# A first block loaded in two halves, its neighbour's statistics on another engine, and a new order of work

## The chip, the cores and the metric

The kernel runs on one core of a Trainium2 chip. Five engines work side by side, each through its own list of instructions in order: TensorE (PE; its weight loads are listed apart as PEld), VectorE (DVE), ScalarE (ACT), GpSimd (POOL) and SyncE (SP), which issues most of the DMA transfers. They wait for each other through semaphores. The metric is the device time of one execution in microseconds (us), the median of several runs.

## What is computed

A layer norm over rows of 640 values feeds two branches, which are added to the input:

```python
x = A_x                                        # (1, 2048, 640)
xn = _layernorm(x, axis=-1)
return x + _A_ref(xn, A_wqkv, A_wo) + _B_ref(xn, B_w1, B_b1, B_w2, B_b2)
```

Branch A is attention with 32 heads of 20 values. Each position sees eight positions: itself and those 2, 4, ... 14 before it; softmax over these eight, weighted sum of the values, then the projection `wo`. Branch B is a dense layer of width 1536 with bias and the tanh form of GELU, and a second dense layer with bias back to 640. Inputs, weights and output are bf16.

## The kernel before

**Tiling.** The 2048 rows are four chunks n = 0..3 of 512 columns (`CH`), each of four blocks of 128 rows (`BPC`). `x_sb` holds the input, block by block. A block is normalised, transposed, and gathered with its neighbours in `xnT`, 5 x 128 features by 512 rows, the moving operand of all projections.

**Layer norm.** Chunks 0 and 1 take mean and variance on VectorE: two half statistics of 320 columns each and one aggregate (`do_st`, L213 and L215). Chunks 2 and 3 take them on ScalarE: a sum (`do_su`, L225), its negative mean (`do_ng`, L229) and a sum of squares (`do_sq`, L232). Block 1 of chunk 0 is taken on ScalarE too, in the pieces `sum1`, `neg1` and `sq1`. `do_rs` (L244, L247) makes the reciprocal root by a logarithm and an exponential on ScalarE. `do_xn` (L264) normalises, for blocks 0 and 1 in two parts of 256 (a) and 384 (b) columns. `do_tp` (L279) transposes on TensorE and `do_tc` (L284) copies the result to `xnT`, on VectorE for block 0 and the first part of block 1, else on ScalarE. From chunk 1 on a DMA transposes (`do_td`, L291).

**Projections.** Chunk 0's are in small pieces: `ga`, `gb2`.. (block 0) and `gd`, `ge` (block 1) for the queries at 128 columns (L346), `hj...` for pairs of blocks at 256 columns (L377), with their copies out of PSUM on ScalarE (`gc.`, `hc...`, L392). Later chunks use `pj` and `pc` at 512 columns (L333, L397).

**Attention.** VectorE multiplies queries with keys (`qk`, L430), folds, and TensorE sums over the values of a head (`lg`, L480). After the softmax SP spreads the weights over partitions by DMA (`xe`, L574), VectorE multiplies with the values (`av`, L581), folds by itself or by an accumulating DMA (`ac`, L592 and L594; `ad`, L598), and writes `oT` (`ot`, L604).

**Dense branch and output.** `f1` (L611) are five matmuls of the hidden layer into one of the four PSUM accumulators of the pool `psA`, `ge` (L627) the GELU. `t` (L690) accumulates the second layer and `wo` for chunks 0 to 2, in parts 0..3 (hidden) and 4 (`wo`); `u` adds the bias, `ut` transposes by DMA, `ud` adds to the output by an accumulating DMA. Chunk 3 is computed the other way round (`o`, L646), with x added by VectorE (`dl`, `dh`) and written in `dd`, `dlo`, `dhi`. Before that `xp` writes x of a whole chunk to the output.

**Order.** The list `ORDER` names every piece of work, and all five engines get their instructions in that order: what stands earlier in the list stands earlier on its engine. It is written out by hand; nothing is reordered afterwards. Loads at the start stand ahead of it: SP issues block 0, the query weights, blocks 2 and 3, the key weights, chunk 1, the value weights and the two halves of w1; ScalarE issues block 1 and the two bias vectors. `ldx` loads the later chunks, `ld2` w2 and `ldo` wo. `tb` (L453) turns the biases on TensorE and `b1` (L456) copies them out. DMA transfers from SP and ScalarE take turns at eight semaphores; a transfer is issued when the eighth before it has landed.

**Warm-up.** Ahead of the list TensorE runs `WARM` matmuls of 512 columns and three of 128 on constants (`do_warm`, L443); the pieces `wa` and `wb` are three more between the first transposes.

Of the kernel before, what the change touches and what calls it, by code (L numbers as in the profile page):

```python
# [29 lines left out]
WARM = 10  # L30
# [13 lines left out]
hj110 xn13 hc112 hj012 tc13 xn11 hj200 hc010 hc110 tc11 qk00 hj011 hc200 hc012 hj201 hc011 xn10 f10_1 hc201 qk02 tc10  # L44
xn12 f10_11 tc12 f10_2 ldx ge0_1 f10_5 qk03 ge0_11 ge0_2 f10_3 ge0_5 f10_0 pad11 ge0_3 pa00 pj103 ge0_0 pj100 pc103
pa01 su20 xp2 pj110 pc100 ld2 pj101 pc110 su22 pb01 pj104 su21 pj102 pc101 su23 pb04 pj114 pc104 ng2 pc102 pj112 ldo
sq22 sq21 lg0 pj111 cp0b cp0a pc112 pj113 mask m0b pc111 pc114 m0a xp1 hj211 pc113 mx0b xp0 mx0a hj210 qk13 ex0a pj122
ex0b hc210 pj123 sq23 ss0b t040 pc122 ss0a sq20 pj124 qk12 hc211 t000 rs2 pc123 f10_4 ri0a pc124 pj120 ri0b at0a rc2
qk11 f10_6 pj121 ge0_4 xn23 f10_7 xn21 qk10 tc23 t041 ge0_6 t001 tc21 pc121 su33 f10_8 pc120 at0b f11_9 su32 pa10 xe00
ge0_7 f11_1 xn20 f11_3 ge0_8 tc20 pa11 xn22 f11_10 ge1_1 tc22 ge1_9 t042 pb11 su31 xe03 t002 xe02 hj202 f10_9 xe01  # L50
hc202 ge1_10 pb14 su30 f10_10 ge0_9 pj203 ge0_10 lg1 pc203 pj210 cp1a av00 cp1b f11_5 ng3 sq32 f11_0 pc210 ge1_5 av01
pj202 ac00 ge1_0 hj212 pc202 pj212 sq30 m1 hc212 pj211 ac01 ge1_3 sq31 av03 t003 pad12 pj222 pc211 pc212 pad21 pj201
mx1 pj220 av02 ex1 t043 pc201 pj224 sq33 pj204 ss1 pc220 pc224 f12_6 pc222 ac03 ri1 pj223 at1 pj214 pc223 ac02 xe10
pc204 pj200 xe13 rs3 pc214 xe12 ad00 pad22 pj213 pc200 xe11 rc3 ad01 f11_6 pc213 xn33 pj221 ot00 xn30 tc33 ot01 f11_8
av10 t004 tc30 t044 u00 t010 av13 u04 ut00 t011 xn32 t012 xn31 tc32 t013 ud00 t014 av11 tc31 ac10 t030 u01 t031 pc221
t032 t033 ac13 ac11 t034 av12 f11_7 t020 t021 ge2_6 t022 ge1_6 ac12 t023 ge1_8 t024 u03 ut01 ad11 f12_9 ot11 pj303
ge2_9 qk22 f11_2 f11_4 ge1_2 pc303 pj301 qk23 ge1_4 f11_11 t130 ge1_11 t131 ad10 ge1_7 f12_2 u02 pc301 ut02 pa21 t140
pad31 ge2_2 pj300 ut03 pj311 ot10 ut04 ud01 f12_3 qk21 pc311 pc300 f13_2 ud02 pj312 xb qk20 pj314 pc312 ud03 pj302
pc314 ge2_3 pj313 pa20 pj304 t132 pc304 pb21 t133 pc302 t134 t141 u13 pb24 f13_5 pj310 ge3_5 ge3_2 lg2 t142 cp2a t143
cp2b t100 pc310 m2 pad32 f13_4 pc313 mx2 t101 qk30 f13_3 ex2 t144 f13_0 ss2 u14 f13_1 qk33 t102 ge3_3 ge3_1 t103 ge3_4  # L60
t110 f13_10 qk31 t104 ri2 f13_8 qk32 ge3_0 pj322 u10 f12_10 ge3_10 t111 at2 ge2_10 f12_8 pa31 pc322 xe22 ut10 f13_6
t112 pa30 f12_5 xe21 xe23 t113 ge2_5 xe20 t120 pb31 ge3_8 f12_0 ge3_6 ge2_8 t114 pb34 f12_4 u11 ut11 ud10 pj321 lg3
pj324 cp3b av21 ge2_4 t121 pc324 t122 cp3a pj323 m3 ac21 f12_7 pc323 mx3 ge2_0 t123 ge2_7 av20 o300 pc321 f13_9 f12_1
ex3 av23 ac20 f13_11 t124 ge2_1 pj320 ac23 u12 ge3_9 ut12 ud11 ud04 f13_7 pc320 ss3 ge3_11 t200 ge3_7 t230 av22 t231
f12_11 ri3 o301 at3 o302 ac22 xe33 ge2_11 t201 xe32 t202 xe31 ad21 t203 ut13 o320 ot21 t232 ad20 o310 o311 ut14 ot20
o312 av33 t204 t233 u20 t234 ut20 av32 t210 u23 ud12 xe30 t211 t212 t213 av31 t220 t221 t214 t222 ac31 u21 t223 t224
av30 t240 u22 ud13 ud20 ut21 ud14 t241 t242 t243 ac30 o330 t244 ac32 o321 u24 ud21 ut22 ad30 ud22 ut23 o331 ut24 o313
ot30 o322 ac33 o303 ud23 o304 ad31 o314 ud24 ot31 dh0 o323 dh1 dl1 o324 dl0 dd1 dd0 o332 dl2 o333 dh2 dd2 o334 ohi dl3
dlo dh3 dhi
# [4 lines left out]
def kernel(  # L74
# [50 lines left out]
    def load_x(b0, b1):  # L125
        nc.sync.dma_start(x_sb[:, b0:b1, :], x_nb[:, b0:b1, :])  # L126
# [12 lines left out]
    load_w(2)  # L139
    for c in range(2):  # L140
        cs = slice(c * F // 2, (c + 1) * F // 2)
        nc.sync.dma_start(w1_sb[:, :, cs], w1_v[:, :, cs])
# [67 lines left out]
    def do_st(n, bl, i):  # L210
# [3 lines left out]
        if i:  # L214
            nc.vector.bn_aggr(mv[:, b, :], stats[:])  # L215
# [635 lines left out]
```

## Time and profile before

| what | us |
|---|---|
| median of 3 runs | 205.6 |
| the runs | 205.41, 205.6, 207.96 |
| the profiled execution | 205.49 |
| its span, first to last instruction | 203.3 |

The span is the part of the execution in which the program's instructions ran; 2.19 us of the profiled execution lie around it. The page gives the busy time of each engine and its share of the span, then the span in slices, the DMA queues, the chain of work that ended last, and the costliest groups of instructions. A busy engine off the chain costs nothing. In a row such as `L611 PE MATMUL hps<-xnT,w_sb ... x240`, L611 is the line of the kernel, `hps` what is written, what follows the arrow what is read; in brackets stands the idle time of the engine before it and what ended that.

### The profile page before, as it was taken

How to read it: one execution, taken by the hardware profiler on the slowest of the kernel's cores; microseconds unless marked ns; L12 is line 12 of the kernel's file. 1: busy time of each engine (PE TensorE's matmuls, PEld its weight loads, DVE VectorE, ACT ScalarE, POOL GpSimd, SP SyncE). 2: the span in 40 equal slices, each digit the busy share in tenths (PEclk: the TensorE clock that was granted, in tenths of full speed). 3: DMA queues.
4: the chain of work that ended last, by engine and by line, in shares of the span. 5: the costliest groups of instructions: out<-in, count | busy, mean ns of one | idle time of the engine just before them, and what ended most of it. 6: DMA issues, size and time to landing. Idle time of an engine off the chain costs nothing.

```text
span 203.3 us, 2874 instructions
## 1 busy us (share of the span) xinstructions
PE 199.4 (98%) x1100; PEld 105.0 (52%) x1100; DVE 185.8 (91%) x159; ACT 129.7 (64%) x237; POOL 29.5 (14%) x35
## 2 busy tenths in 40 slices
PE   8999999999999999999999999999999999999994
PEld 3899455654454555444444544444444445444552
DVE  2899999899997999999999996999979999999981
ACT  5689979999979897555545437697447990211100
POOL 3000000000000400024202500000202702253420
PEclk9999999999999999999999999999999999999999
DMA  6996399940673681849912890001863898895951
GB/s 204 390 395 208 77 355 336 348 148 3 91 155 89 110 148 22 219 92 163 193 17 52 102 99 5 3 0 15 170 98 69 153 118 147 111 120 90 103 90 64
DMA packets 38430, 27.31 MB, mean 134 GB/s; under 512 B 25106, under 2 KB 34578, under 8 KB 38418
## 3 DMA queue, kind: packets, MB, share of 16 engines
q1 hardware_dynamic: 28016, 20.29, 38.2%
q0 software_dynamic: 10080, 6.56, 26.3%
q10 hardware_dynamic: 322, 0.30, 0.4%
q8 instruction: 8, 0.13, 0.3%
q14 instruction: 4, 0.03, 0.0%
HBM read 10.49 MB, written 4.59 MB: 74 GB/s over the span
## 4 chain that ended last, share of the span: by engine, by line
PE 96%; DMA 2%; SPq 0%; DVE 0%; issue 0%
PE T L690 27%; PE hps L611 25%; PE pps L333 24%; PE lo L646 7%; PE gps L377 7%; DMA wq_sb<-in_A_wqkv_dram 2%; PE hi L646 2%; PE gps L346 1%; PE L L480 1%; PE tp L279 0%; SPq L126 0%; DVE prod L658 0%; PE tb L453 0%
## 5 line engine op out<-in xcount | busy, mean ns | idle before, releaser
L611 PE MATMUL hps<-xnT,w_sb 128*128 128x512 bf16 x240 | 56.9, 379 | 0.0
L430 DVE TENSOR_TENSOR prod<-qT,kT 128x5120 bf16<-128x5120 bf16 x16 | 44.5, 2820 | 0.1
L690 PE MATMUL T<-hT,w_sb 128*128 128x512 bf16 x180 | 43.4, 379 | 0.0
L611 PEld LDWEIGHTS <-w_sb 128*128 128x128 bf16 x240 | 23.5, 98 | 27.5
L702 POOL DMA_DIRECT2D out_dram<-x_sb x15 | 20.9, 1492 | 87.5 <-DMA x_sb<-x_sb 87.5
L627 ACT ACTIVATE hT<-hps,bT 128x512 bf16<-128x512 f32 x36 | 23.9, 689 | 12.1 <-PE hps L611 9.6
L690 PEld LDWEIGHTS <-w_sb 128*128 128x128 bf16 x180 | 17.5, 98 | 21.1 <-issue 0.4
L693 ACT ACTIVATE x_sb<-T,bT 128x512 bf16<-128x512 f32 x15 | 10.3, 688 | 25.6 <-PE T L690 24.5
L581 DVE TENSOR_TENSOR prod<-vT,ax 128x5120 bf16<-128x5120 bf16 x8 | 22.4, 2820 | 2.7 <-PE L L480 1.5
L581 DVE TENSOR_TENSOR prod<-vT,x_sb 128x5120 bf16<-128x5120 bf16 x8 | 22.2, 2817 | 0.0
L592 POOL DMA_DIRECT2D prod<-prod x6 | 7.8, 1300 | 77.5 <-DVE prod L581 77.5
L170 ACT ACT_TABLE_LOAD x14 | 18.0, 1283 | 1.0 <-PEq L835 0.7
L471 DVE TENSOR_TENSOR prod<-prod 128x4096 bf16<-128x4096 bf16 x8 | 18.3, 2291 | 0.3
L333 PE MATMUL pps<-xnT,wv_sb 128*128 128x512 bf16 x75 | 18.5, 379 | 0.0
L690 PE MATMUL T<-oT,wo 128*128 128x512 bf16 x75 | 18.5, 379 | 0.0
L333 PE MATMUL pps<-xnT,wq_sb 128*128 128x512 bf16 x75 | 18.1, 379 | 0.0
L465 DVE TENSOR_TENSOR prod<-prod 128x4096 bf16<-128x4096 bf16 x8 | 18.0, 2286 | 0.0
L333 PE MATMUL pps<-xnT,wk_sb 128*128 128x512 bf16 x75 | 18.0, 380 | 0.0
L594 DVE TENSOR_TENSOR prod<-prod 128x2560 bf16<-128x2560 bf16 x10 | 14.8, 1487 | 0.1
L333 PEld LDWEIGHTS <-wq_sb 128*128 128x128 bf16 x75 | 8.8, 117 | 7.5
L333 PEld LDWEIGHTS <-wv_sb 128*128 128x128 bf16 x75 | 8.7, 118 | 7.6 <-issue 0.4
L333 PEld LDWEIGHTS <-wk_sb 128*128 128x128 bf16 x75 | 8.6, 118 | 7.7 <-issue 0.8
(91 smaller groups left out, 242.6 us busy)
## 6 DMA issues: line engine op xcount, KB each, us to landing
prod<-prod POOLq DMA_DIRECT2D x6, 640.0 KB, 6.8
ax<-attn SPq DMA_DIRECT2D x8, 256.0 KB, 3.9
x_sb<-attn SPq DMA_DIRECT2D x8, 256.0 KB, 4.5
w_sb<-in_B_w_dram SPq DMA_DIRECT2D x2, 960.0 KB, 11.0
out_dram<-x_sb SPq DMA_DIRECT2D x3, 640.0 KB, 6.8
w_sb<-in_B_w_dram SPq DMA_DIRECT2D x4, 480.0 KB, 6.6
out_dram<-x_sb POOLq DMA_DIRECT2D x15, 128.0 KB, 5.6
x_sb<-in_A_x_dram SPq DMA_DIRECT2D x2, 640.0 KB, 7.0
```

What stands on the lines that cost most here:

```text
L170: nc.scalar.preload_act_table_set(name)
L333: nc.tensor.matmul(ps[:], lhsT=wqkv_p[which][:, ti, to, :], rhs=xnT[:, ti, :], start=(ti == 0), stop=(ti == KT - 1),)
L430: nc.vector.tensor_tensor(out=prod[:, j], in0=q[:, :, at].unsqueeze(1).to_broadcast([P, W, KT, P]), in1=window(k, at), op=ALU.mult,)
L465: nc.vector.tensor_tensor(out=low, in0=low, in1=high, op=ALU.add)
L471: nc.vector.tensor_tensor(out=first, in0=first, in1=rows[:, :, t * P : (t + 1) * P], op=ALU.add)
L581: nc.vector.tensor_tensor(out=prod[:, j], in0=window(qkv_tile(n, 2), slice(j * P, (j + 1) * P)), in1=ax_view(n)[:, j, :, :].unsqueeze(2).t ...
L594: nc.vector.tensor_tensor(out=low, in0=low, in1=high, op=ALU.add)
L611: nc.tensor.matmul(ps[:], lhsT=w1_sb[:, ti, ft * P : (ft + 1) * P], rhs=tiles["xnT", n][:, ti, :], start=(ti == 0), stop=(ti == KT - 1),)
L627: nc.scalar.activation(hT, tiles["hps", n, ft][:], ACT.Gelu_apprx_tanh, bias=bT[:, ft : ft + 1], scale=1.0)
L646: nc.tensor.matmul(out_ps(bl, hi), lhsT=lhs, rhs=rhs[:, CH:D] if hi else rhs[:, 0:CH], start=pc == 0 and k == 0, stop=pc == 4 and k == len ...
L690: nc.tensor.matmul(ps[:], lhsT=lhs, rhs=rhs, start=pc == 0 and k == 0, stop=pc == 4 and k == len(srcs) - 1)
L702: nc.gpsimd.dma_start(dst, src, accum_op=ALU.add)
```

## The change

- Block 0 is loaded in two transfers of 320 columns each, both from SP.
- Block 1's statistics are taken on VectorE like its neighbours': the pieces `sum1`, `neg1`, `sq1` go, `st01a`, `st01` and, on its own in the order, the aggregate `ag01` come. Its normalisation subtracts the mean as the others do.
- The two bias loads move from ScalarE's queue to SP's, behind the value weights.
- Block 0's second copy to `xnT` and block 1's first move from VectorE to ScalarE.
- w2 is loaded in three transfers instead of four.
- The hidden matmuls of chunk 0 are split into pieces of two and three (`f10_..a`, `f10_..b`), which accumulate into the same tile.
- Nine warm-up matmuls instead of ten.
- Another order. Its first lines, and the stretches in which the attention weights of chunk 0 are spread, are shown; the rest is a different interleaving of the same pieces.

```diff
-WARM = 10
+WARM = 9
 ORDER = """
-pad01 pad02 st00a st00 sum1 rs00 neg1 xn00a sq1 xn00b tp00a wa tp00b tc00a wb rs01 tc00b ga xn01b gb2 xn01a tp01b
-st03a tp01a tb tc01b gb3 tc01a gb4 st03 gd gc0 st02a ge rs03 st02 hj101 xn03 rs02 gc1 xn02 tp03 gc4 st12a tp02 tc03
-hj100 st13a st13 tc02 st12 hj102 hc101 st11a hj111 hc100 st10a hc102 st11 hj010 st10 hc111 ho b1 rs1 hj112 pk rc1 qk01
+pad02 pad01 st00a st00 st01 rs00 xn00a st01a tp00a wa wb xn00b ag01 tc00a tp00b rs01 ga tc00b xn01a xn01b gb2 st03a
+tp01a tp01b gb3 st03 tc01a gb4 tc01b gd st02a rs03 st02 ge ho xn03 rs02 hj101 gc0 xn02 gc1 tp02 gc4 tp03 st13a hc101
+hj102 st11a tc03 st11 hj100 tc02 st13 st12a hj010 hc100 st12 hc102 st10a tb hj110 st10 hc010 b1 rs1 hj012 hc110 rc1
...
-qk11 f10_6 pj121 ge0_4 xn23 f10_7 xn21 qk10 tc23 t041 ge0_6 t001 tc21 pc121 su33 f10_8 pc120 at0b f11_9 su32 pa10 xe00
-ge0_7 f11_1 xn20 f11_3 ge0_8 tc20 pa11 xn22 f11_10 ge1_1 tc22 ge1_9 t042 pb11 su31 xe03 t002 xe02 hj202 f10_9 xe01
+hj202 ge0_8 f10_6a tc20 f10_6b xn23 t001 hc202 tc23 ge1_1 f10_10a at0a pa11 f10_10b ge0_6 f11_3 ge0_10 xn22 f10_9a
+pa10 f10_9b xn21 tc22 f11_9 tc21 f11_10 ge1_9 at0b pb11 xe00 t002 ge1_10 xe03 pj124 ge1_3 xe01 su33 pj121 pb14 su32
+xp1 t042 su31 xe02 pj203 ge0_9 pc121 lg1 su30 hj212 av00 t003 ng3 pc124 pj212 cp1b hc212 pc203 f11_5 sq32 av01 ac00
...
-    load_x(0, 1)
+    for cs in (slice(0, D // 2), slice(D // 2, D)):
+        nc.sync.dma_start(x_sb[:, 0, cs], x_nb[:, 0, cs])
     nc.scalar.dma_start(x_sb[:, 1, :], x_nb[:, 1, :])
-    nc.scalar.dma_start(b_rt[0:FT, :], B_b1.rearrange("(t p) -> t p", p=P))
-    nc.scalar.dma_start(b_rt[FT : FT + KT, :], B_b2.rearrange("(t p) -> t p", p=P))
     load_w(0)
     load_x(2, BPC)
     load_w(1)
     load_x(BPC, 2 * BPC)
     load_w(2)
+    nc.sync.dma_start(b_rt[0:FT, :], B_b1.rearrange("(t p) -> t p", p=P))
+    nc.sync.dma_start(b_rt[FT : FT + KT, :], B_b2.rearrange("(t p) -> t p", p=P))
...
-        for c in range(4):
-            ts = slice(c * FT // 4, (c + 1) * FT // 4)
+        for c in range(3):
+            ts = slice(c * FT // 3, (c + 1) * FT // 3)
...
-        if i:
-            nc.vector.bn_aggr(mv[:, b, :], stats[:])
+        if i and b != 1:
+            do_ag(b)
+
+    def do_ag(b):
+        nc.vector.bn_aggr(mv[:, b, :], tiles["stats", b][:])
...
-            scalar1=neg[:, 1:2] if bl == 1 else mv[:, i, 0:1],
+            scalar1=mv[:, i, 0:1],
             scalar2=rstd[:, i : i + 1],
-            op0=ALU.add if bl == 1 else ALU.subtract,
+            op0=ALU.subtract,
             op1=ALU.mult,
...
-    def do_f1(n, ft):
-        ps = psA.tile([P, CH], F32, tag="acc", name="hps")
-        tiles["hps", n, ft] = ps
-        for ti in range(KT):
+    def do_f1(n, ft, a=0, b=KT):
+        ps = get(("hps", n, ft), lambda: psA.tile([P, CH], F32, tag="acc", name="hps"))
+        for ti in range(a, b):
...
-    for u, a, b, eng in (("a", 0, 2, "ve"), ("b", 2, KT, "se")):
+    for u, a, b, engs in (("a", 0, 2, ("ve", "se")), ("b", 2, KT, ("se", "se"))):
         for bl in range(2):
             piece(f"xn0{bl}{u}", do_xn, 0, bl, a, b)
             piece(f"tp0{bl}{u}", do_tp, 0, bl, a, b, True)
-        piece(f"tc00{u}", do_tc, 0, 0, a, b, "ve")
-        piece(f"tc01{u}", do_tc, 0, 1, a, b, eng)
+        for bl in range(2):
+            piece(f"tc0{bl}{u}", do_tc, 0, bl, a, b, engs[bl])
```

The later lines of the order end alike, with `ohi dl3 dlo dh3 dhi`.

More of the change, by code (lines that the diff above doesn't have):

```diff
@@ new lines @@
+pj202 cp1a sq30 pj201 pc212 pc202 pj214 ge1_5 m1 ac01 sq31 t043 av03 pc201 f11_0 pc214 pj200 ge1_0 pj222 mx1 av02
+pj211 ex1 pj210 pc211 pad12 pc200 pj221 ss1 sq33 pj213 pc221 ac02 pc210 pj223 ri1 rs3 at1 pj220 pc213 rc3 ac03 xe12
+pc222 xn30 pj224 xe11 xe13 ad00 pc223 f11_7 pc220 xn31 ad01 f11_4 pc224 tc31 f12_6 ot00 ot01 pj204 tc30 av12 t004
+pc204 xe10 t044 u00 pad21 xn32 t010 av13 t011 u04 ut00 xn33 t012 t013 tc33 ud00 t030 av11 t014 tc32 t031 u01 t032 t020
+av10 ac11 t021 ge1_4 f11_11 t022 ge1_11 ac13 t033 ac10 ge1_7 t034 ac12 xb t023 u03 ut01 t024 ad11 pj303 ot11 f11_2
@@ L70 @@
+t224 o313 ad31 u22 ud13 ud20 ut21 ud14 t240 av31 t241 t242 o330 t243 t244 ac30 o331 u24 ud21 ut22 ud22 ut23 ac31 o320
+ut24 o321 ot31 o322 ud23 ad30 o323 o324 ot30 ud24 o303 dh2 o314 o304 dl1 dl2 o332 dh1 dd2 dh0 dl0 o333 dd1 dd0 o334
+ohi dl3 dlo dh3 dhi
 """.split()
@@ L241, in do_rs @@
         sl = slice(n * BPC + b0, n * BPC + b1)
-        summed = n in ACT_STATS or (n, b0) == (0, 1)
         table(LOG_SET)
         nc.scalar.activation(
-            logv[:, sl], mv[:, sl, 1], ACT.Ln, bias=eps_t[:], scale=1.0 / D if summed else 1.0
+            logv[:, sl], mv[:, sl, 1], ACT.Ln, bias=eps_t[:], scale=1.0 / D if n in ACT_STATS else 1.0
         )
@@ L720 @@
             piece(f"tp0{bl}{u}", do_tp, 0, bl, a, b, True)
-        piece(f"tc00{u}", do_tc, 0, 0, a, b, "ve")
-        piece(f"tc01{u}", do_tc, 0, 1, a, b, eng)
+        for bl in range(2):
+            piece(f"tc0{bl}{u}", do_tc, 0, bl, a, b, engs[bl])
     for bl in range(BPC):
-        if bl != 1:
-            piece(f"st0{bl}a", do_st, 0, bl, 0)
-            piece(f"st0{bl}", do_st, 0, bl, 1)
+        piece(f"st0{bl}a", do_st, 0, bl, 0)
+        piece(f"st0{bl}", do_st, 0, bl, 1)
         piece(f"rs0{bl}", do_rs, 0, bl, bl + 1)
@@ L791 @@
         for ft in range(FT):
-            piece(f"f1{n}_{ft}", do_f1, n, ft)
+            if n:
+                piece(f"f1{n}_{ft}", do_f1, n, ft)
+            else:
+                piece(f"f1{n}_{ft}a", do_f1, n, ft, 0, 2)
+                piece(f"f1{n}_{ft}b", do_f1, n, ft, 2, KT)
             piece(f"ge{n}_{ft}", do_ge, n, ft)
```

44 lines of the change are left out of this document (17 added, 27 removed).

## The prediction

> **What bounds the kernel now.** I read the page's busy times and its chain first, then the busy times by window, then the first microseconds engine by engine, then the places where another engine hands work to TensorE.
>
> ```profile
> PE 199.4 (98%) x1100; PEld 105.0 (52%) x1100; DVE 185.8 (91%) x159; ACT 129.7 (64%) x237; POOL 29.5 (14%) x35
> ...
> PE 96%; DMA 2%; SPq 0%; DVE 0%; issue 0%
> ```
>
> TensorE (PE) is busy for 98% of the span and makes up 96% of the chain that ended last; VectorE (DVE) is second at 91%. By stage (window, its length, then busy time of PE, weight loads, DVE, ScalarE and GpSimd; the last figure is GB/s of the DMA engines):
>
> ```profile
> 0.00:6.31 6.31, 5.17 (x21) 2.10 (x22) 2.19 (x7) 3.82 (x9) 1.53 (x13) 1.00 0.71 238
> 6.31:200.60 194.29, 194.24 (x1079) 102.93 (x1079) 183.31 (x152) 125.92 (x229) 27.93 (x22) 1.00 0.66 132
> 200.60:203.30 2.70, 0.00 (x0) 0.00 (x0) 0.29 (x1) 0.00 (x0) 0.00 (x0) 0.89 0.20 61
> sum 203.30, PE 199.41 PEld 105.04 DVE 185.79 ACT 129.74 POOL 29.46; mean PE 66.47 PEld 35.01 DVE 61.93 ACT 43.25 POOL 9.82
> ```
>
> From 6.31 to 200.60 PE idles for 0.05 us in all. So the time is a head of 6.31 us, 194.3 us of PE work without a hole, and a tail of 2.7 us. The change takes none of that work away: the one matmul that goes is a warm-up on constants in the head. A gain can come only from the head or the tail, and the last steps of the tail stand in both orders alike; a loss comes as a later head or as a hole in the middle. Two per cent of 205.6 us is 4.1 us, about what a measurement of this kernel can tell from no change.
>
> What ends the head, from the chain in order of time (start, length, what):
>
> ```profile
> 1.19 5.07 DMA wq_sb<-in_A_wqkv_dram
> 6.27 0.05 issue
> 6.31 1.03 PE gps L346 x15
> ...
> 9.64 1.09 PE gps L377 x10
> 10.73 0.56 PE tp L279 x10
> ```
>
> The first real matmuls wait for the query weights, issued at 1.19 and landed at 6.26.
>
> **The head, step by step.** SP's own rows, VectorE's, ScalarE's and those of PE's weight loads (start, length, engine, line, operation, and in brackets the idle time before it and its releaser):
>
> ```profile
> 0.74 0.39 SPq L126 DMA_DIRECT2D x_sb<-in_A_x_dram  x1
> 1.19 0.42 SPq L129 DMA_DIRECT2D wq_sb<-in_A_wqkv_dram  x1
> ...
> 3.65 0.85 SPq L129 DMA_DIRECT2D wv_sb<-in_A_wqkv_dram  x1
> 6.28 2.23 SPq L142 DMA_DIRECT2D w_sb<-in_B_w_dram  x2
> ```
>
> ```profile
> 3.27 0.89 DVE L213 BATCH_NORM_STATS2 stats<-x_sb 128x6 f32<-128x320 bf16 x2 [3.27 <-DMA x_sb<-in_A_x_dram]
> 4.19 0.21 DVE L215 BATCH_NORM_AGGREGATE mv<-stats 128x2 f32<-128x12 f32 x1
> 5.07 0.63 DVE L264 TENSOR_SCALAR xn<-x_sb,mv,rstd 128x256 bf16<-128x256 bf16 x2 [0.66 <-ACT rstd L247]
> 5.79 0.70 DVE L284 COPY xnT<-tp 128x256 bf16<-128x256 bf16 x2
> ```
>
> ```profile
> 3.65 0.74 ACT L225 ACTIVATE trash<-x_sb 128x640 bf16<-128x640 bf16 x1 [1.63 <-DMA x_sb<-in_A_x_dram]
> 4.29 0.19 ACT L225 ACTIVATION_READ_ACCUMULATOR trash<-x_sb 128x1 f32 x1
> 4.50 0.29 ACT L244 ACTIVATE logv<-mv,eps_t 128x1 f32<-128x1 f32 x1
> ...
> 7.55 0.48 ACT L284 COPY xnT<-tp 128x384 bf16<-128x384 bf16 x1 [0.91 <-PE tp L279]
> ```
>
> ```profile
> 4.15 0.15 PEld L443 LDWEIGHTS <-const-bfloat16-1.0 128*128 128x128 bf16 x1 [0.28 <-issue]
> ...
> 6.31 0.77 PEld L346 LDWEIGHTS <-wq_sb 128*128 128x128 bf16 x13 [0.28 <-DMA wq_sb<-in_A_wqkv_dram]
> ```
>
> *Two column halves.* No row shows a load of half a block. The whole block, issued at 0.74, let the statistics begin at 3.27, 2.53 later. The first half carries half the bytes and can hardly be later; the second is issued one place later, by the step from 0.74 to 1.19, 0.45. It lands between 3.27 (the same bytes by the same time) and 3.72. Before, the second statistic began half of 0.89 after the first, at about 3.7; now it begins between 3.5 (the first half at best some 0.25 sooner) and 3.75. I take 3.6, nearer to the whole block's row. ScalarE gains a little as well: block 1's sum and its read-out held it until 4.48, while the aggregate was there at 4.40, so the logarithm starts some 0.05 sooner. Block 0's first normalised columns come at 5.07 - 0.15 = 4.9, with bounds of 4.75 and 5.05.
>
> The Trainium skill's page "DMA: Bandwidth & Descriptors", section "Anatomy of one DMA", speaks against halving: about 2.0 us fixed for each transfer, plus bytes / 436e3, fitted on the gpsimd path. That makes an estimate of 2.4 us for the 160 KB block (the trace has 2.53 to its first use) and 2.2 for a half: the second half would be there at 3.4, and the head below would come out 0.15 shorter.
>
> *The query weights, one issue later.* They go out at about 1.64. If the landing follows the issue, it moves from 6.26 to 6.71; if the transfers ahead of it keep the DMA engines busy anyway, it stays. The engines moved 238 GB/s averaged over the whole head, its idle start included, against 132 over the rest, so I lean to the second and take 6.4.
>
> *Block 1's statistics on VectorE.* ScalarE's sum and square go; VectorE gets two half statistics (0.45 each) and an aggregate (0.21). The first half statistic stands before the normalisation, inside VectorE's wait of 0.66, and is free while that wait lasts (0.45 if it went). The other half statistic and the aggregate stand between the first normalisation and the copy that fills xnT: 0.66 in line. From the start of the normalisation to the end of the first copy it took 5.79 + 0.35 - 5.07 = 1.05 and will take 1.7, so the copy ends at 4.9 + 1.7 = 6.6, with bounds of 6.45 and 6.75. So a new wait, for VectorE's copy, comes 0.2 behind the weights. First projection at 6.6 instead of 6.31: +0.3.
>
> *The second copy moves to ScalarE*, behind block 1's logarithm and exponential. Those wait for the aggregate (6.25), take 0.55 up to what reads them (from 4.50 to 5.07), and the copy 0.48: columns at 7.3. Ten of the fifteen projections (1.03 for 15) cover 6.6 to 7.3. No further loss, 0.1 at most.
>
> *Warm-up.* A warm-up matmul steps at 0.15 + 0.28 = 0.43 us; one less is worth nothing, since PE waits behind them for the normalised columns. The second rival has its other side.
>
> Sum of the head: +0.3, with bounds of -0.05 (the weights at 6.26) and +0.45.
>
> **Moves that should cost nothing.** The bias loads leave ScalarE's queue for SP's, behind the value weights and ahead of w1. Landing times by issue:
>
> ```profile
> w_sb<-in_B_w_dram SPq DMA_DIRECT2D x2, 960.0 KB, 11.0
> ...
> wv_sb<-in_A_wqkv_dram SPq DMA_DIRECT2D x1, 800.0 KB, 9.3
> ```
>
> The value weights land at 3.65 + 9.3 = 12.95, the biases (17 rows of 128 values) behind them, by my estimate between 13.0 and 13.6. The matmul that turns them has been moved behind four groups of key and query matmuls and ten transposes: from 9.64, 35 x 0.109 (1.09 for 10) + 0.56 = 4.4, so to 14.0 and with the later head 14.3. PE does not wait; if the biases came as late as w1 does, PE would wait up to 3 us there. w1's issue waited until 6.28, when the query weights had landed; two short issues fit in front of that. w1's second half is now used first, at about 20; the halves land 11.0 after issue in the median, about 17.3, and with an issue up to 1.1 later 18.4. The hidden projections of the first chunk split into 2 + 3 matmuls, the same number; one accumulator of four is held longer at one place, which I price at nothing to 0.2. w2 in three loads moves the same bytes.
>
> **The middle.** The new order is another interleaving; only waits decide. The tightest place that I find is the spreading of the first attention weights by SP:
>
> ```profile
> 53.44 0.68 SPq L574 DMA_DIRECT2D ax<-attn  x1
> 55.13 2.59 SPq L291 DMA_TRANSPOSE xnT<-xn  x2
> ```
>
> ```profile
> 63.31 5.56 DVE L581 TENSOR_TENSOR prod<-vT,ax 128x5120 bf16<-128x5120 bf16 x2 [1.21 <-ACT qT L397]
> ```
>
> ```profile
> 83.45 1.55 DVE L604 TENSOR_TENSOR oT<-prod 128x1280 bf16<-128x1280 bf16 x2
> ```
>
> ```profile
> 85.44 2.32 PE L690 MATMUL T<-oT,wo 128*128 128x512 bf16 x10
> ```
>
> ```profile
> DMA to landing us min/median/max: 3.6/4.3/7.2
> ```
>
> Before, the first of these loads left at 53.44, ahead of two transposes, and the product that reads it began at 63.31, about 5.5 us after it had landed. In the new order all four transposes stand ahead of it, so it leaves at 55.13 + 2.59 = 57.7 and lands at 62.0 by the median of 4.3: 1.3 ahead of its product if VectorE keeps its time. Covered, but thinly. One output write is also moved between the third and the fourth of these loads; the fourth's product is now the last of four and comes some 8 us later, which covers it.
>
> So the middle adds nothing, and the profiled execution, 205.49 us with a span of 203.3, becomes 205.8. The median of the three runs, 205.6, stands 0.1 above it; the forecast is 205.9.
>
> **Rivals.**
> 1. *The head does not lose.* The halves land early, the weights at 6.26, VectorE's copy by 6.4: -0.05 to +0.1, and up to 0.25 less where another thin wait goes; 205.3 to 205.7. For it: PE waited 0.28 for the weights with its columns nearly there. Against it: 0.66 us of VectorE work put in line.
> 2. *TensorE starts its real work at half speed.* In the stream a matmul of 512 columns takes 6.47 / 30 = 0.216 us:
>
> ```profile
> 20.65 6.47 PE hps L611 x30
> ```
>
>    The warm-ups step at 0.43, twice that; the first projections, 1.03 / 15 = 0.069 for 128 columns, are near a quarter of 0.216. So PE changed to full speed during the warm-up or just behind it. If with nine the change comes after the real work began, the first fifty projections take up to 50 x 0.069 = 3.4 us more, some of it hidden in waits: 206.5 to 209. Each microsecond of half speed after 6.6 costs 0.5; over 2% takes 8 of them. For it: 0.43 less warm-up. Against it: the change had come within ten. The Trainium skill, "TensorE: Matmul & The Clock Gate", Part 1, says that the gate opens after about 3.4 us of busy time in a window that runs free of the kernel; by it nine warm-ups (3.9 us) leave the window less room than ten, and the outcome would differ between runs.
> 3. *VectorE waits for the attention weights.* If the load takes the 7.2 of the slowest row, it lands at 64.9, 1.6 late. VectorE's oT products end at 85.0 and PE takes them at 85.44, so 0.4 of that is covered and PE idles up to 1.2 us: 206.3 to 207.1. It decides from a landing after 63.7. This and the second end slower than before.
>
> **How the numbers follow.** Forecast (head +0.1 to +0.45, middle whole; 205.6 to 206.2): 0.60. Rival 1: 0.19. Rival 2: 0.08. Rival 3: 0.07. Another hole in the new order, which I did not find, of any size: 0.06. The range takes the forecast, rival 1 and rival 3, down by 0.3 and up by 0.2 for what separates runs: 205.0 to 207.3. Faster by over 2% would need 4.1 us, where PE's idle time in the head is 6.31 - 5.17 = 1.14: 0.01. Slower by over 2%, from half of the unfound holes and the far end of rival 2: 0.05. Within: 0.94.
>
> **What would show it.** Right: first projection at 6.5 to 6.7, released by VectorE's copy; first normalisation at 4.75 to 5.05; no PE hole beyond; first spreading load at about 58. Wrong: a first projection before 6.4 (rival 1); 128-column matmuls over 0.1 us each after 6.6 (rival 2); VectorE idle for the attention weights, or PE near 85 (rival 3); PE waiting at the bias matmul near 14.

## The result and the profile after

| | before | after |
|---|---|---|
| median us (22 runs each) | 205.41 | 207.61 |
| fastest run | 205.28 | 205.89 |
| profiled execution, span | 205.49, 203.3 | 207.85, 205.8 |

The ratio is 1.0077 with a 95% interval of 1.0053 to 1.0101: slower, by less than 2%. It compares the means without the one run of each kernel at 213 and more; the medians alone give 1.0107. The 22 runs of the changed kernel fall into two groups: nine from 205.89 to 206.81, twelve from 207.50 to 208.35 (and one at 213.95). The groups are groups of the TensorE clock: the mean clock granted over the run was 0.999 to 1.000 in each of the nine and 0.990 to 0.992 in each of the twelve. The profiled one, at 0.991, belongs to the upper group.

The page's busy times and TensorE's granted clock over 40 slices of the span:

```profile
PE 199.4 (97%) x1080; PEld 106.3 (52%) x1099; DVE 186.0 (90%) x160; ACT 125.8 (61%) x232; POOL 29.4 (14%) x35
...
PEclk9799999999999999999999999999999999999999
```

TensorE is as busy as before, in a longer span, and the clock dips in the second slice (5 to 10 us). The chain of waits of the changed kernel (start, length, what):

```profile
1.66 5.68 DMA wq_sb<-in_A_wqkv_dram
7.39 1.74 PE gps L350 x15
9.12 0.53 PE tp L283 x5
9.65 2.62 PE gps L350 x35
12.28 1.09 PE gps L381 x10
```

The chain of before had the same five steps. The first projection now starts at 7.39 instead of 6.31, 1.08 later. The fifteen projections take 1.74 instead of 1.03, and the ten key matmuls start at 12.28 instead of 9.64: 2.64 later, of which 1.08 is the late start and 1.56 slower work. The span grew by 2.5, so the whole loss lies in the first 12 us. PE's waits in the whole span (what it waited for, us in total, times, the longest) are three, and all lie ahead of 7.39:

```profile
PE gps L350 <- DMA wq_sb<-in_A_wqkv_dram: 1.1, 1, 1.1
PE tp L283 <- DVE xn L268: 0.8, 2, 0.6
PE idle L447 <- PEq L839: 0.8, 1, 0.8
```

The 1.08 is shown by PE's timeline (in brackets the idle time and its releaser):

```profile
5.97 0.34 PE L283 MATMUL tp<-ident,xn 128*128 128x128 bf16 x3 [0.23 <-DVE xn L268]
7.39 1.74 PE L350 MATMUL gps<-xnT,wq_sb 128*128 128x128 bf16 x15 [1.08 <-DMA wq_sb<-in_A_wqkv_dram]
```

The 1.56 is shown by the windows of the changed kernel, cut where the trace records a change of the clock; the last but two figure is the granted clock, the last the GB/s of the DMA engines. Ahead of the first recorded change the view shows a clock of 1.00, though the warm-ups step at half speed there:

```profile
3.00:4.00 1.00, 1.00 (x4) 0.31 (x3) 0.86 (x2) 0.00 (x0) 0.00 (x0) 1.00 0.40 83
4.11:7.52 3.41, 1.51 (x15) 0.85 (x14) 2.40 (x9) 1.36 (x5) 0.00 (x0) 1.00 1.03 357
7.52:10.93 3.41, 3.41 (x34) 3.41 (x34) 2.50 (x8) 1.49 (x7) 0.00 (x0) 0.50 1.06 394
```

and of the kernel before:

```profile
3.00:4.00 1.00, 1.00 (x4) 0.32 (x3) 0.73 (x2) 0.35 (x1) 0.00 (x0) 1.00 0.91 289
4.73:8.14 3.41, 3.05 (x46) 2.42 (x43) 2.75 (x9) 2.26 (x8) 0.00 (x0) 1.00 1.06 387
```

In both, the warm-up brought the full clock before the real work: at 4.11 and at 4.73. In the next 3.41 us PE was busy for 3.05 before, and the clock stayed full. In the changed kernel it was busy for 1.51, waiting for more than half of the time, and the following 3.41 us ran at half clock, all of it real work. Half speed for 3.41 us is a loss of 1.7, near the 1.56 found, and takes 1.7 / 206 = 0.008 off the mean clock, as the runs of the upper group have it.

The first rows of both windows hold the other half of the story: between 3 and 4 us, about when the first statistics on block 0 begin (2.87 here, 3.27 before), the DMA engines moved 83 GB/s instead of 289.

### The profile page after: what moved, and what is told of

It is laid out like the page before. It is cut to its first block, busy times and chain, and to the rows that moved or that the text cites. A ratio compares the mean times of both kernels' runs of the same rounds, so it can differ in the third digit from the quotient of the medians.

```text
span 205.8 us, 2843 instructions
## 1 busy us (share of the span) xinstructions
PE 199.4 (97%) x1080; PEld 106.3 (52%) x1099; DVE 186.0 (90%) x160; ACT 125.8 (61%) x232; POOL 29.4 (14%) x35
## 4 chain that ended last, share of the span: by engine, by line
PE 95%; DMA 3%; issue 1%; SPq 0%; DVE 0%
PE T L693 27%; PE hps L614 25%; PE pps L337 24%; PE lo L649 7%; PE gps L381 7%; DMA wq_sb<-in_A_wqkv_dram 3%; PE gps L350 2%; PE hi L649 2%; PE L L484 1%; PE tp L283 1%; SPq L133 0%; DVE prod L661 0%; PE tb L457 0%
## 5 line engine op out<-in xcount | busy, mean ns | idle before, releaser
L614 PE MATMUL hps<-xnT,w_sb 128*128 128x512 bf16 x236 | 55.5, 379 | 0.2
L693 PE MATMUL T<-hT,w_sb 128*128 128x512 bf16 x176 | 43.9, 379 | 0.2
L596 POOL DMA_DIRECT2D prod<-prod x6 | 7.3, 1211 | 80.3 <-DVE prod L585 80.3
L337 PE MATMUL pps<-xnT,wv_sb 128*128 128x512 bf16 x72 | 18.0, 379 | 0.2
L401 ACT CAST qT<-pps 128x512 bf16<-128x512 f32 x15 | 8.9, 591 | 8.4 <-PE pps L337 8.4
```

Source lines behind the costliest of these rows:

```text
L337: nc.tensor.matmul(ps[:], lhsT=wqkv_p[which][:, ti, to, :], rhs=xnT[:, ti, :], start=(ti == 0), stop=(ti == KT - 1),)
L614: nc.tensor.matmul(ps[:], lhsT=w1_sb[:, ti, ft * P : (ft + 1) * P], rhs=tiles["xnT", n][:, ti, :], start=(ti == 0), stop=(ti == KT - 1),)
L693: nc.tensor.matmul(ps[:], lhsT=lhs, rhs=rhs, start=pc == 0 and k == 0, stop=pc == 4 and k == len(srcs) - 1)
```

## The experiments

Theory A: the query weights, issued behind the second half of block 0, come late (1.08); and TensorE, idle for that time, loses its clock for 3.41 us in those executions in which the cut between two such windows falls badly (1.6 more), which makes the two groups. Against it stood: B, VectorE's added statistics hold the first projection; C, the new order loses in the middle; D, nine warm-ups are too few by themselves. Later the first part of A was split: is it the halving, the place in the queue, or the later issue?

The readings of all profiles in one table. "Issued" is SP's issue of the query weights, "GB/s" what the DMA engines moved between 3 and 4 us, "landed after" the time from that issue to the weights' landing; then the first projection; then how long PE was busy in its first 3.41 us at full clock, and the clock behind it; then the runs. What each kernel is stands in the parts below, which carry the names.

| kernel | issued | GB/s | landed after | first projection | busy of 3.41 | clock behind | runs us | ratio (95%) |
|---|---|---|---|---|---|---|---|---|
| before | 1.19 | 289 | 5.1 | 6.31 | 3.05 | full | 205.28 fastest |  |
| after | 1.66 | 83 | 5.7 | 7.39 | 1.51 | half | 205.89 fastest | 1.0077 (1.0053-1.0101) |
| a_whole | 1.19 | 344 | 4.5 | 6.37 | 2.85 | full | 205.37-210.14 | 1.0040 (0.9995-1.0085) |
| a_act | 1.18 | 237 | 5.6 | 7.47 | 1.81 | half | 205.34-209.23 | 1.0042 (1.0004-1.0080) |
| a_fill | 1.66 | 62 | 6.4 | 8.98 | 1.55 | half | 206.14-209.54 | 1.0043 (1.0010-1.0076) |
| b_half | 1.66 | 46 | 6.8 | 8.51 | 1.33 | half | 206.69-209.99 | 1.0075 (1.0039-1.0110) |
| a_third | 1.66 | 131 | 5.8 | 7.47 | 1.55 | half | 206.61-209.54 | 1.0122 (1.0082-1.0162) |
| a_rows | 2.02 | 117 | 5.7 | 7.80 | 1.68 | half | 208.53-208.70 | 1.0153 (1.0140-1.0166) |
| a_tiny | 1.61 | 144 | 6.3 | 7.99 | 1.84 | full | 207.07-209.72 | 1.0159 (1.0127-1.0191) |
| a_warm | 1.66 | 69 | 6.1 | 7.79 | 2.89 | full | 206.12-207.25 | 1.0059 (1.0042-1.0076) |
| b_nine | 1.19 | 312 | 4.9 | 6.35 | 3.41 | full | 205.25-206.10 | 1.0005 (0.9991-1.0018) |
| b_six | 1.19 | 298 | 5.8 | 7.05 | 3.41 | full | 206.47-206.91 | 1.0056 (1.0036-1.0075) |
| best | 1.19 | 364 | 4.6 | 6.43 | 3.28 | full | 205.92-207.29 | 1.0031 (1.0016-1.0045) |
| best_fill | 1.19 | 314 | 5.6 | 6.80 | 2.96 | full | 206.13-206.61 | 1.0039 (1.0026-1.0051) |

a_whole, a_act, a_fill and b_half ran on a chip on which the kernel before itself went from 205.20 to 210.44 in 35 runs. Their ratios say little; they are read by their profiles, their fastest runs and the mean clock of each run.

### Block 0 whole again (a_whole)

```diff
-    for cs in (slice(0, D // 2), slice(D // 2, D)):
-        nc.sync.dma_start(x_sb[:, 0, cs], x_nb[:, 0, cs])
+    load_x(0, 1)
```

> The kernel after, with block 0 loaded whole again, so that the query weights are issued second on SP's queue. Theory A (the loss is the late query weights, 7.34 instead of 6.26, and behind it a TensorE clock that falls to half for 3.4 us in about half of the runs): the weights are issued near 1.2 and land near 6.3, the first projection starts at 6.3 to 6.7, no window of half clock after it, 205.3 to 205.9 in all runs, no second group above 207. Theory B (VectorE's added statistics in line hold the first projection): the columns come no earlier than before, first projection at 6.6 or later, released by VectorE, 205.8 to 206.2. Theory C (the new order loses in the middle) and theory D (one warm-up less is enough to lose the clock): time as the kernel after, near 207.6 with both groups.

The weights were there 4.5 after an issue at 1.19, and the first projection started at 6.37, with no wait for them. Windows of this kernel:

```profile
3.00:4.00 1.00, 1.00 (x4) 0.32 (x3) 0.77 (x2) 0.00 (x0) 0.00 (x0) 1.00 1.00 344
5.14:8.55 3.41, 2.85 (x44) 2.55 (x45) 2.93 (x11) 1.68 (x6) 0.00 (x0) 1.00 1.06 393
```

The DMA engines are full between 3 and 4 us again, the clock stays, the profiled span is 203.4 against 203.3 before. Everything else of the change is still in this kernel, VectorE's statistics, the new order and nine warm-ups among it. So in this execution these cost about 0.1 together, and B and C are out as causes of more than that; D, which is about some executions only, is left to the runs with fewer warm-ups below. "All runs" was a miss: seven of twelve stood above 207.8. Six of these seven had a mean clock of 0.984 to 0.992, so the clock fell in them although the weights were issued early; in the same call it fell in six of 35 runs of the kernel before. None of the seven was profiled, and whether the weights were late in them stays open. On other chips kernels with the weights issued at 1.19 kept it: `b_nine` in ten runs of ten, `best` in twelve of twelve (0.998 or more).

### The kernel before, with two halves (b_half)

The two lines of the diff above, the other way round, in the kernel before.

> The kernel before, with nothing changed but block 0 loaded in two column halves on SP's queue. Theory A: the weights are issued near 1.65 and land at 6.7 to 7.4, the first projection follows them, and a half clock shows in some runs: +0.5 to +1.1 in the runs with a full clock, +2 to +2.6 in the others; with ten warm-ups, perhaps fewer of the latter than in the kernel after. Theories B, C, D: 205.4, as the kernel before.

Even the fastest run, 206.69, is 1.49 above the fastest of the kernel before in that call. The weights came 6.8 after their issue, PE waited 1.6 for them, and the clock fell in spite of ten warm-ups. The halving alone, in the old kernel, brings the loss. In four of the twelve runs the mean clock was 0.989 to 0.990; in the other eight, that fastest one among them, it was 1.000, so time is lost at full clock as well. Four of twelve against twelve of 21 in the kernel after, on another chip, are too few to say that the tenth warm-up makes the fall rarer.

The weights were not the only late load. VectorE waited for the second half of block 0, issued at 1.19, until 4.40:

```profile
4.40 0.49 DVE L214 BATCH_NORM_STATS2 stats<-x_sb 128x6 f32<-128x320 bf16 x1 [1.28 <-DMA x_sb<-in_A_x_dram]
```

The normalised columns began at 5.80 here, 0.73 later than with the block whole, and PE waited 1.1 for them ahead of its 1.6 for the weights.

### The second half from ScalarE's queue (a_act)

```diff
-    for cs in (slice(0, D // 2), slice(D // 2, D)):
-        nc.sync.dma_start(x_sb[:, 0, cs], x_nb[:, 0, cs])
+    nc.sync.dma_start(x_sb[:, 0, 0 : D // 2], x_nb[:, 0, 0 : D // 2])
+    nc.scalar.dma_start(x_sb[:, 0, D // 2 : D], x_nb[:, 0, D // 2 : D])
```

> The kernel after, with the second half of block 0 issued from ScalarE's queue ahead of block 1: the halving stays, SP's extra issue goes. Theory A with the place in the queue as the cause: the weights are issued near 1.2 and land at 6.3 to 6.5, first projection at 6.4 to 6.7, 205.3 to 206.0. Theory A with the halving itself as the cause (the data engines run dry between 3 and 4 us because the block comes as two short transfers): the weights land at 6.8 or later although they are issued near 1.2, and some runs show the half clock. Theories B, C, D: as the kernel after, near 207.6.

The weights kept their place and their issue at 1.18, and took 5.6 all the same: they landed at 6.8, as expected if the halving itself were the cause, and the clock fell in four runs of twelve (mean clock 0.990 to 0.992), the profiled one among them. The next two kernels are needed to judge that cause. Here the weights did not even bound: block 1, now second in ScalarE's queue, came at 5.71, and VectorE stood waiting for it with the first normalisation queued behind (the row of VectorE's timeline):

```profile
5.73 0.49 DVE L215 BATCH_NORM_STATS2 stats<-x_sb 128x6 f32<-128x320 bf16 x1 [1.60 <-DMA x_sb<-in_A_x_dram]
```

So in this execution the added issue delayed the transfer behind it on ScalarE's queue. It isn't so in each: the fastest runs, 205.34 and 205.39, leave no room for it.

### Block 0 and block 1 whole, both from SP; and a tiny load in the second half's place (a_third, a_tiny)

```diff
-    for cs in (slice(0, D // 2), slice(D // 2, D)):
-        nc.sync.dma_start(x_sb[:, 0, cs], x_nb[:, 0, cs])
-    nc.scalar.dma_start(x_sb[:, 1, :], x_nb[:, 1, :])
+    load_x(0, 1)
+    load_x(1, 2)
```

> The kernel after with block 0 loaded whole and block 1 moved to SP's queue behind it: the query weights are third in SP's queue, as in the kernel after, and no transfer is halved. Theory P (the place in the queue makes the weights late): issued near 1.65, they land at 6.6 or later, and the first projection waits for them. Theory H (the halving makes them late: two short transfers leave SP's queue nearly empty between 3 and 4 us): they land at 5.7 to 6.4 although they are third, the first projection starts at 6.4 to 6.7 behind VectorE's copy, fastest run 205.3 to 205.7.

The second kernel keeps block 1 on ScalarE's queue, and has the lines marked + in place of the two halves:

```diff
+    load_x(0, 1)
     nc.scalar.dma_start(x_sb[:, 1, :], x_nb[:, 1, :])
+    nc.sync.dma_start(b_rt[FT : FT + KT, :], B_b2.rearrange("(t p) -> t p", p=P))
     load_w(0)
```

> The kernel after with block 0 loaded whole, block 1 on ScalarE's queue, and the small bias load (5 rows of 256 bytes) moved to SP's queue between block 0 and the query weights: the weights are third in SP's queue and issued 0.4 to 0.5 later, but almost no bytes stand between. Theory P1 (the later issue is what counts: the first blocks have landed before the weights' packets are under way, the data engines run half empty between 3 and 4 us, and the weights take 5.7 to 6.8 from issue to landing): they land at 6.9 to 8, the first projection waits for them, fastest run 206 or more. Theory P2 (it counts that another block's bytes stand in the same queue): issue near 1.65, 4.5 to 5.1 to landing as with the blocks on two queues, so 6.2 to 6.8; first projection at 6.4 to 6.8, fastest run 205.3 to 205.8.

Windows and chain of the first, then of the second:

```profile
3.00:4.00 1.00, 1.00 (x5) 0.33 (x4) 0.87 (x2) 0.00 (x0) 0.00 (x0) 1.00 0.73 131
```

```profile
1.66 5.76 DMA wq_sb<-in_A_wqkv_dram
7.47 1.79 PE gps L349 x15
```

```profile
3.00:4.00 1.00, 1.00 (x4) 0.31 (x3) 0.69 (x2) 0.00 (x0) 0.00 (x0) 1.00 0.64 144
5.78:9.19 3.41, 1.84 (x29) 1.50 (x27) 1.62 (x7) 0.88 (x4) 0.00 (x0) 1.00 1.05 380
```

```profile
1.61 6.33 DMA wq_sb<-in_A_wqkv_dram
7.99 1.03 PE gps L349 x15
```

Nothing is halved in either, and in the second only 1.2 KB stand ahead of the weights that were not there before. Still the weights are as late as in the kernel after. This is theory P1 as expected: one more issue ahead of the weights, which moves theirs to 1.6, is enough. Theory H (that it takes a halving) and P2 (that it takes a block's bytes ahead) fall; the halving needs no other cost than the issue that it puts in front of the weights. What these runs do not separate is the later time of the issue from the third place in SP's queue: the late kernels have both. The table bears the reading out over all fourteen profiles. The seven kernels that issued the weights at 1.6 or later moved 46 to 144 GB/s between 3 and 4 us; those that issued them at 1.2 with block 0 whole moved 289 to 364, and a_act 237. Nothing lies between 144 and 237. It isn't only that everything happens 0.4 to 0.8 later in the seven: in the second that begins 1.81 after the weights' issue, as 3.00 does after an issue at 1.19, they moved 84 to 223, against 237 to 364. From issue to landing the late ones took 5.7 to 6.8, the others 4.5 to 5.8; these overlap, so an early issue alone does not make a load fast (b_six took 5.8, best_fill 5.6).

The second kernel also corrects theory G below: its clock stayed full behind a window with 1.84 us busy, so its profiled loss is the late weights alone: 1.7 at the first projection (7.99 against 6.31) and 1.8 in the span (205.1 against 203.3). Its three other runs had a mean clock of 0.984 to 0.992 and were 1.2 to 2.7 slower.

### Two halves of rows instead of columns (a_rows)

```diff
-    for cs in (slice(0, D // 2), slice(D // 2, D)):
-        nc.sync.dma_start(x_sb[:, 0, cs], x_nb[:, 0, cs])
+    for rs in (slice(0, P // 2), slice(P // 2, P)):
+        nc.sync.dma_start(x_sb[rs, 0, :], x_nb[rs, 0, :])
```

> The kernel after with block 0 loaded in two halves of 64 rows, each row whole (1280 bytes), instead of two halves of the columns (640 bytes of each row): same number of transfers, same places in the queue, same bytes, pieces as long as in the kernel before. If it is the number of transfers or the place: the weights are as late as in the kernel after, 7.3 to 8.5. If it is the short pieces: they land at 5.7 to 6.7. All 128 rows are there when the second transfer has landed, near 3.3 to 3.7, so the first statistic may start 0.3 later than in the kernel after.

The short pieces are not the cause: with pieces of 1280 bytes the weights took 5.7 as well, and SP needed 1.24 to issue the two halves where the column halves took 0.87, so they came at 7.7. VectorE's first statistic, expected 0.3 later, came at 4.66, 1.8 later. So here the normalised columns were as late as the weights: PE waited 1.75 for them ahead of its first transposes. By its median the slowest kernel of the study, and its four runs all lost the clock (mean 0.990 to 0.992).

### The clock: filling TensorE's idle time (a_fill, a_warm)

```diff
+    piece("wc", do_warm, 20, P)
```

with `wc` between `tp00b` and `rs01` in the order.

> The kernel after, with 20 more warm-up matmuls of 128 columns on constants behind block 0's last transposes, where TensorE would wait for the query weights. Theory A: the weights land as late as in the kernel after (near 7.3), the first projection starts at 7.4 to 7.6, but TensorE is busy until then and the clock stays full: one group of runs, 206.0 to 206.7, and none above 207; the first fifty projections at about 0.07 each. If the clock falls for another reason than the idle time ahead of the first projection: the two groups stay, near 206.3 and 207.9. Theory D (too little warm-up ahead of 6 us, whatever comes later): the two groups stay as well.

By the times this was a miss: six of twelve runs stood above 207. By the clock it was half a hit: only two of the twelve, at 208.46 and 209.54, had lost it (mean 0.992), and what made the other four slow, up to 208.27 at a clock of 1.000, is not known. The profiled execution is one of the two, and shows how the clock could still fall. In it the full clock came at 3.44 and its 3.41 us ended at 6.85, where the added matmuls only began (6.85); PE had been busy for 1.55 of them, because the normalised columns came late. The fill stood behind the idle time that mattered, then ran at half speed and held up the first projection to 8.98, when the weights had landed at 8.1. The next kernel fills both places:

```diff
-WARM = 9
+WARM = 12
-    piece("wb", do_warm, 2, P)
+    piece("wb", do_warm, 4, P)
+    piece("wc", do_warm, 14, P)
```

> The kernel after with 12 warm-up matmuls instead of 9, four instead of two small ones between block 0's transposes, and 14 small ones behind them. Theory G (the clock falls for one window of 3.41 us when TensorE was busy for less than some two thirds of the window of full clock before it: 3.05 and 2.85 us busy kept it, 1.81, 1.55, 1.51 and 1.33 did not): TensorE is busy for over 2.6 us of any such window, no half clock behind the warm-up in any undisturbed run, one group of runs at 206.0 to 206.8 (the weights are still late). Otherwise (the fall comes from something else than idle time): a group some 1.5 us above it remains, with about half of the runs.

As theory G expects: the weights are as late as ever (6.1, first projection at 7.79), PE is busy for 2.89 of 3.41, the clock stays, and the fifteen projections take 1.03 as in the kernel before:

```profile
7.79 1.03 PE L350 MATMUL gps<-xnT,wq_sb 128*128 128x128 bf16 x15 [0.53 <-DMA wq_sb<-in_A_wqkv_dram]
```

All six runs kept the clock (mean 0.998 to 1.000), and the highest is 207.25, where thirteen of 22 of the kernel after stood above 207.4. What is left, 1.0059, is the late weights and, in the profile, 0.2 us at the bias matmul, whose loads come later with everything on SP's queue; three runs lie up to 0.45 above the expected group. So the clock's part of the loss goes when idle time is filled, without any change to the loads.

### The warm-up alone (b_nine, b_six)

The kernel before with `WARM = 9`, and with `WARM = 6`.

> The kernel before with nine warm-up matmuls instead of ten, nothing else. Theory G: the real work starts at 6.31 as before, the window of full clock holds 0.2 to 0.4 us less busy time, fastest run 205.2 to 205.4, at most a few more runs in the upper group than the kernel before has in the same call. Theory D (one warm-up less is what loses the clock in the kernel after): half of the runs near 207 or above.

> The kernel before with six warm-up matmuls instead of ten, nothing else; the weights come as in the kernel before, so the real work can start at 6.3. Theory G: no window ahead of 6.3 is busy enough, or the one behind it isn't; the first projections run at half speed (0.11 each or more, against 0.069) for 1.5 to 5 us, and nearly all runs stand 0.7 to 2.6 above the kernel before. If the half clock in the kernel after came from the late weights in another way than through idle time: 205.3 to 205.6.

Nine cost nothing (1.0005, interval 0.9991 to 1.0018; mean clock 0.998 or more in all ten runs), so D falls. With six the span is 1.4 longer:

```profile
7.05 1.79 PE L346 MATMUL gps<-xnT,wq_sb 128*128 128x128 bf16 x15 [0.56 <-DVE xn L264]
```

The clock became full only at 8.94, and the first fifteen projections took 1.79, 0.76 more. The other 0.7 is a later start, which the warm-up does not explain. The row names VectorE as the releaser, but in this execution the weights landed at 1.19 + 5.8 = 7.0, so it was they.

### A kernel to beat both (best, best_fill)

On top of block 0 whole: VectorE copies block 0's first columns ahead of block 1's second half statistic, and TensorE does all of block 0's query projections ahead of block 1's transposes.

```diff
-pad02 pad01 st00a st00 st01 rs00 xn00a st01a tp00a wa wb xn00b ag01 tc00a tp00b rs01 ga tc00b xn01a xn01b gb2 st03a
-tp01a tp01b gb3 st03 tc01a gb4 tc01b gd st02a rs03 st02 ge ho xn03 rs02 hj101 gc0 xn02 gc1 tp02 gc4 tp03 st13a hc101
+pad02 pad01 st00a st00 st01 rs00 xn00a tp00a wa wb xn00b tc00a st01a ag01 tp00b tc00b ga rs01 gb2 xn01a xn01b gb3 gb4 st03a
+tp01a tp01b st03 tc01a tc01b gd st02a rs03 st02 ge ho xn03 rs02 hj101 gc0 xn02 gc1 tp02 gc4 tp03 st13a hc101
```

The second kernel has `WARM = 11` and `wb` of three besides.

> The kernel after with block 0 loaded whole, and on VectorE the copy of block 0's first columns ahead of block 1's second half statistic and aggregate, on ScalarE the second copy ahead of block 1's logarithm, on TensorE all of block 0's query projections ahead of block 1's transposes. With the weights landed at 5.7 to 6.3, the first projection starts at 6.0 to 6.3 instead of 6.37, and nothing is late behind it: fastest run 204.9 to 205.2, against 205.2 to 205.3 of the kernel before. If the first projection follows the weights' landing anyway: 205.2 to 205.4. Runs in which the clock falls stand some 1.7 higher.

> The kernel of the run before with 11 warm-up matmuls instead of nine and three small ones instead of two between the transposes. Theory G (a window of 3.41 us with less than some two thirds of TensorE's time busy loses the clock): fewer runs in the upper group than without the added ones, and the fastest run within 0.2 of it, later where the warm-ups hold up the first transposes: 205.0 to 205.4.

Neither beats the kernel before (1.0031 and 1.0039). The first projection came at 6.43, not at 6.0 to 6.3: in this execution the clock was half until 6.52, so the transposes ahead of the copy ran slowly. And something was late behind it. Block 1's normalisation, VectorE's rows of the first kernel:

```profile
6.76 0.21 DVE L219 BATCH_NORM_AGGREGATE mv<-stats 128x2 f32<-128x12 f32 x1
7.62 0.64 DVE L267 TENSOR_SCALAR xn<-x_sb,mv,rstd 128x256 bf16<-128x256 bf16 x2 [0.65 <-ACT rstd L250]
```

It began at 7.62 against 6.76 with block 0 whole alone. Block 1's aggregate, now behind VectorE's copy, began at 6.76 instead of 5.97, and that accounts for 0.79 of the 0.86. The logarithm began at 7.05, 0.08 after the aggregate's end, so ScalarE's copy ahead of it cost no more than that. The first key matmul came at 10.33 instead of 9.82. That accounts for 0.5 of 0.9 in the span; the rest is not traced. The second is no faster. Whether its warm-ups guard the clock is not shown, since neither kernel lost it in any run (mean 0.998 or more in all 21).

## What held of the prediction and what failed, by its own steps

The forecast was 205.9 with a range up to 207.3. The median is 207.61, 0.3 beyond the range; 205.6 times the ratio of 1.0077 is 207.2, just inside it. Either way the upper end of the range was not there for what happened: it was taken from rival 3, and neither did VectorE wait for the attention weights nor PE near 85. So an end inside the range would be luck. "Slower by less than 2%" held, and 22 runs told 0.8% from no change, where the prediction took 2% for the least that can be told.

**The query weights, one issue later: the step that failed.** It took their landing at 6.4, with bounds of 6.26 and 6.71; measured 7.34 (1.66 + 5.68). The first projection, forecast at 6.6 and released by VectorE's copy, came at 7.39 and was released by the weights. The upper bound assumed that the time from issue to landing stays 5.07. It does not: over the fourteen profiles it went from 4.5 to 6.8, and none of the seven with a later issue took less than 5.7. The step took 238 GB/s, averaged over the head of the kernel before, for a sign that the engines stay busy in the new one. Between 3 and 4 us they moved 289 GB/s before and 83 after. Of the 1.08, 0.47 is the later issue (1.66 against 1.19) and 0.6 the slower transfer.

**Half speed, which the sum put at nothing.** Rival 2 gave 206.5 to 209 with a chance of 0.08. The upper group lies in there, and its sign showed: 128-column matmuls of 1.74 / 15 = 0.116 us. It had the size and not the mechanism, for it looked for the full clock coming too late, with nine warm-ups. The clock came in time, at 4.11, and was lost again because PE idled; nine warm-ups in the kernel before cost nothing. The text priced the warm-up as "worth nothing, since PE waits behind them", and did not ask what the wait itself does to the clock. Given the true landing, the two groups can be estimated: between the end of the warm-up and the first projection PE is busy for 0.8 us, and a busy time of 1.84 kept the clock, so some 1.04 of projections must fall into the window, which then begins no earlier than 7.39 - 3.41 + 1.04 = 5.0 (somewhat earlier counts too, as the last warm-ups then run in it). In the profiles it began anywhere from 3.44 to 6.52 (apart from six warm-ups), so about half of the executions lose; twelve of 22 did. With the first projection at 6.31 the same sum gives 3.9, and few do. What the prediction drew from the Trainium skill, "TensorE: Matmul & The Clock Gate", Part 1, that the outcome would differ between runs, came true.

**Block 1's statistics on VectorE: size too large, and it never decided.** The first copy was to end at 6.6; it ended at 6.18. VectorE's rows of the changed kernel:

```profile
2.87 1.10 DVE L215 BATCH_NORM_STATS2 stats<-x_sb 128x6 f32<-128x320 bf16 x2 [2.87 <-DMA x_sb<-in_A_x_dram]
...
4.88 0.35 DVE L268 TENSOR_SCALAR xn<-x_sb,mv,rstd 128x256 bf16<-128x256 bf16 x1 [0.31 <-ACT rstd L251]
5.14 0.49 DVE L215 BATCH_NORM_STATS2 stats<-x_sb 128x6 f32<-128x320 bf16 x1
5.55 0.36 DVE L268 TENSOR_SCALAR xn<-x_sb,mv,rstd 128x384 bf16<-128x384 bf16 x1
5.82 0.20 DVE L220 BATCH_NORM_AGGREGATE mv<-stats 128x2 f32<-128x12 f32 x1
5.94 0.24 DVE L288 COPY xnT<-tp 128x256 bf16<-128x256 bf16 x1
```

Back to back, the statistic holds the engine for 5.55 - 5.14 = 0.41 and the aggregate for 0.12, not 0.45 and 0.21; and part of the 1.05 taken from before had been the copy waiting for the transposes (5.47 + 0.28 = 5.75, copy at 5.79). So from the start of the normalisation to the end of the copy it took 1.30 (6.18 - 4.88), where 1.7 was forecast.

**Right:** the first normalisation at 4.88 (4.9 forecast, 4.75 to 5.05). The second copy on ScalarE with no loss; its columns were there at 6.96, against 7.3:

```profile
6.50 0.46 ACT L288 COPY xnT<-tp 128x384 bf16<-128x384 bf16 x1
```

The bias matmul ran at 16.49 without a wait: 14.3 plus the later start (7.39 - 6.6) and the 1.56 of half clock would be 16.6. The middle whole: the first three attention-weight loads went out from 60.39, 57.9 when the 2.5 are taken off, against 57.7, and no PE wait followed.

**Right in this profile, and in part by luck: the two halves.** The first half of block 0 was in use 2.87 - 0.74 = 2.13 after its issue. The estimate of 2.2 from the Trainium skill, "DMA: Bandwidth & Descriptors", section "Anatomy of one DMA", agrees with that. VectorE's first normalised columns came 0.2 sooner than before, but PE waited for the weights and not for them. And the gain is not in each execution: the second half, put between 3.27 and 3.72, was waited for until 4.19 in `a_fill` and 4.40 in `b_half`, 3.0 and 3.2 after its issue, and the first normalisation then began at 5.59 and 5.80 instead of 5.07.

## What to carry to other kernels

At the start of this kernel an added small transfer was paid by the one behind it: measure when the bytes that release the first real work land, and look at the DMA rate second by second, not at an average over the stage. Where TensorE is the bound, idle time ahead of the real work can cost twice, here 1.08 for the wait and 1.56 for a spell of half clock behind a spell that was busy for 1.51 of 3.41 us. A kernel whose runs fall into two groups is to be profiled in both, or judged by the share of runs in each, since one profile shows only one of them; the mean clock of each run tells them apart.

## What the runs showed of the hardware

- At full clock, each spell of 3.41 us decided the clock of the next. Busy times of 2.85 us and more kept it, and so did 1.84; 1.81, 1.68, 1.55, 1.51 and 1.33 lost it. The expectation of "two thirds" was too high for this: by these profiles the limit, if busy time as the profile models it is the right measure, lies just over half. To gain the full clock took more: 2.02 us of warm-ups in the spell ahead of 2.80 in `b_nine` and 2.33 ahead of 3.11 in `best` did not bring it, 2.66 ahead of 3.44 in `a_fill` did.
- The Trainium skill, "TensorE: Matmul & The Clock Gate", section "HAM oscillation — how this bites in real kernels", warns of idle gaps over about 3.4 us. Here the longest single gap was 1.08 us and the clock fell, while a gap of 1.45 us in `a_tiny` was survived, so the measurement decides: it is the sum over the spell that counts.
- When a spell begins has no relation to the program: thirteen of the profiles have 3.44, 3.77, 4.11, 4.53, 4.73 and so on to 6.52, with TensorE's first matmul at 0.78 in all of them. The Trainium skill's page "TensorE: Matmul & The Clock Gate", Part 1, calls the window free-running, and these runs agree.
- With one issue of 1.2 KB in front of it, a load of 800 KB landed at 7.94 (`a_tiny`) instead of 5.7 (`a_whole`) and 6.26 (the kernel before). Why the DMA engines fall to half of their rate and less between 3 and 4 us when that issue is 0.4 later is not settled by these runs.
